# Transposing the attention weights on VectorE and through DRAM instead of on TensorE, from the fourth batch on

## The chip, the cores and the metric

The kernel runs on one NeuronCore of a Trainium2 chip. A core has a matrix engine (TensorE, "PE" in the profile; its weight loads are "PEld"), three engines for elementwise work (VectorE "DVE", ScalarE "ACT", GpSimd "POOL") and SyncE ("SP"), whose queue here issues nearly all transfers (DMA). The engines run their own instruction streams in order and wait for each other by semaphores. TensorE writes its results to PSUM, a small memory of banks; the other engines read them from there.

The metric is the device time of one execution in microseconds (us), as a median of several runs. One further execution was recorded by the hardware profiler; all times of single instructions come from it.

## The reference

All numbers are float32. There are 8 batches, 8 heads, 576 tokens and a head width of 64.

```
scores = q @ k^T / 8
attn   = exp(scores - max) where scores >= max - tau, else 0;   attn /= sum(attn)
x      = attn @ v, heads put side by side: 576 x 512 for each batch
u      = x + real(fft over tokens (fft over channels (x)))
out    = u + relu(layernorm(u) @ w_ch1) @ w_ch2          (512 -> 2048 -> 512)
```

## The kernel before

**Attention** goes by pairs of heads: 4 pairs a batch, 32 in all (`n`). The queries of a pair are cut into five steps: t = 0 to 3 have 128 queries of both heads, and t = 4 has the last 64 queries of each head, 128 rows together. So there are 20 steps a batch and 160 in all (`i`). A step computes scores on TensorE into two double banks of PSUM (tag "sc"), the negated row maximum on VectorE (L506), the exponential on ScalarE (L512), the threshold and the row sum in one VectorE instruction (L527), and, from the third batch on, scales the weights by the reciprocal sums on ScalarE (L540).

The product with v contracts over the keys, so it needs the weights with keys on the partitions. The function `weights_in_parts` does this: TensorE transposes each 128 x 128 piece of the weights `e` into PSUM (one instruction at L578 for the 64 last keys of both heads, eight at L596), and ScalarE copies the results to `e_t` and `ends` (L584, L598). For t = 4 there are five transposes, since its 128 rows share one set of keys.

`values_in_parts` then multiplies: part 0 takes the queries of t = 0 and 1, part 1 those of t = 2, 3 and 4. Each part is 20 recorded matmuls (L627).

**The mixing** (the Fourier transforms, folded by symmetry) and **the feed-forward** run behind, a batch at a time. The feed-forward takes groups of 512 tokens. From the second group on both products use a two-level fast scheme with fewer block products (Strassen's kind); their weight forms are made once, kept in DRAM (`f1`: 28 blocks, `f2`: 49 blocks of 256 KB) and streamed in for each of these eight groups. They come through a ring in the tiles `w1[0..2]`: a load takes `PER` blocks, `block` asks for a later load when it reaches the first block of one, and `ensure` issues it on SyncE's queue (L1036).

**The order** is written out by hand. From step 40 on one loop (L1635) runs the steps: scores of step `i`; values of a part; maxima and exponentials; a piece of filling (`fill`); thresholds and reciprocals; the transposes of step `i - 1`, with two more pieces of filling in and behind them; scaling of the weights. A piece of filling is mixing and feed-forward work for a fixed number of matmul columns. This number, `per_slot`, is set once a batch from the work that is left. What remains of the feed-forward runs after the last step. At t = 3 VectorE prepares q and k of the next pair by 32 x 32 block transposes (`prep_pair`, L398 to L401), at t = 2 its v is loaded, and at the end of t = 4 q and k of the pair after next are (L134: eight transfers of 72 KB in runs of 128 bytes). At the end of each batch, VectorE folds the rows of the last pair.

`mm` is a set of four PSUM banks that all other matmuls and the transposes share in turn. Each bank has to be emptied by ScalarE or VectorE before TensorE can use it again.

The code that the change touches, with what calls it:

Of the kernel before, what the change touches and what calls it, by code (L numbers as in the profile page):

```python
# [47 lines left out]
def kernel(  # L48
# [18 lines left out]
    NT = 5  # L67
# [29 lines left out]
    v_in = [const.tile([128, 10, D], FP32, name=f"v_in{u}") for u in range(2)]  # L97

# [158 lines left out]
    w1 = [const.tile([128, HID], FP32, name=f"w1_{c}") for c in range(ND)]  # L257
# [181 lines left out]
    def softmax(i, between=None, meanwhile=None, behind=None):  # L439
# [43 lines left out]
        if normalized(i // NT):  # L483
            nc.vector.tensor_scalar(
                out=e[:, 0:S], in0=e[:, 0:S], scalar1=den[:, 0:1], scalar2=None, op0=ALU.mult
            )
            if nh == 2:
                nc.scalar.activation(
                    out=e[:, S : 2 * S], in_=e[:, S : 2 * S], func=ACT.Copy, scale=den[:, 1:2]
                )  # L490
        else:
            rec = sb.tile([128, 2 * D], FP32, tag="rec", name="rec")
            nc.gpsimd.tensor_copy(
                rec[:, :].rearrange("p (j d) -> p j d", j=nh), _repeated(den[:, 0:nh], 2 * D // nh)
            )
# [51 lines left out]

    def transposed_weights(i):
        for _ in weights_in_parts(i):
            pass  # L550

    def weights_in_parts(i):

        n, t = divmod(i, NT)
        e, rec = steps.pop(i)
        if t in (0, 2):

            e_t = sb.tile([128, 8, S - 256], FP32, tag="e_t", bufs=1, name="e_t")  # L560
            ends = sb.tile([128, 2, S - 256], FP32, tag="ends", bufs=1, name="ends")
            vt = heads[n][2]
            if t == 0 and PAIRS[n % NPAIR] % 2:

                vt = sb.tile([128, 10, D], FP32, tag="vr", bufs=1, name="v_rev")
                src = heads[n][2]
                nc.gpsimd.tensor_copy(vt[:, :, 0:1], src[:, :, 0:1])
                last = src[:, :, D - 1 : D]
                down = bass.AP(
                    tensor=last.tensor, offset=last.offset,  # L570
                    ap=[list(last.ap[0]), list(last.ap[1]), [-1, D - 1]],
                )
                nc.gpsimd.tensor_copy(vt[:, :, 1:D], down)
            heads[n] = (*heads[n][0:2], vt, e_t, ends)
# [5 lines left out]
        if rec is not None:  # L580
            nc.tensor.transpose(pe[:, 1, :], rec[:, :], ident[:, :])
            kept = 2
# [22 lines left out]
    def values_in_parts(n, part):  # L605
# [19 lines left out]
        for c in range(5):  # L625
            for j in range(2):
                nc.tensor.matmul(  # L627
                    pv[64 * j : 64 * j + 64, 0:m], vt[:, 2 * c + j, :],
                    e_t[:, 4 * j + c, 0:m] if c < 4 else ends[:, 0, 0:m],
                    start=(c == 0), stop=(c == 4), skip_group_check=True,  # L630
                )
        yield
        if normalized(n):
# [238 lines left out]
    def channels(rows):  # L872
# [18 lines left out]
        def both():  # L891
            yield from w1_forms()
            ensure(1)
            while not next(forms_w2):
                yield
# [32 lines left out]
    def w1_forms():  # L928
# [36 lines left out]
        ensure(0)  # L965
# [60 lines left out]
    PER = 4  # L1026
    LOADS = [(f1, 28, k) for k in range(0, 28, PER)] + [(f2, 49, k) for k in range(0, 49, PER)]
    issued = 0

    def ensure(n):  # L1030

        nonlocal issued
        while issued <= n and issued < (NG - 1) * len(LOADS):
# [3 lines left out]
                out=w1[issued % 3][:, 0 : 512 * n_blocks].rearrange("p (j n) -> p j n", n=512),  # L1037
# [4 lines left out]
    def block(g, second, index):  # L1042

        n = len(LOADS) * (g - 1) + (7 if second else 0) + index // PER
        if index % PER == 0:
            ensure(n + 2 if g > 1 or second or index < 20 else n + 1)
        return w1[n % 3][:, 512 * (index % PER) : 512 * (index % PER + 1)]

# [586 lines left out]
    for i in range(2 * per_batch, total + 3):  # L1635
# [6 lines left out]
        if t == 3 and i < total:  # L1642
# [8 lines left out]
        next(values, None)  # L1651
        if i % per_batch == 2:
# [6 lines left out]
        while held:  # L1659
            held.pop(0)()  # L1660
        if mixes:
# [82 lines left out]
```

## Time and profile before

| | |
|---|---|
| median of three runs | 1605.9 us (1603.56 to 1607.93) |
| profiled execution | 1605.7 us, span from first to last instruction 1603.8 us |
| busy in it | PE 1537.4, PEld 1189.2, DVE 1105.6, ACT 908.4, POOL 811.7 us |
| mean granted TensorE clock | 0.988 of full speed |
| transferred | 239.05 MB, 149 GB/s over the span |
| transposes into `pw` (L596) | 1152 instructions, 172.1 us busy |
| their copies to `e_t` (L598) | 256 instructions, 148.5 us busy |

The page of the profile lists the engines' busy time, then the span in 40 slices (each digit is a busy share in tenths), the transfer queues, the chain of work that ended last, the costliest groups of instructions, and the transfers. A group's line names the source line, engine and operation, output and inputs, shapes and count; then the busy time in us and the mean ns of one; then how long its engine sat idle just before them, and what ended that wait. Busy time of overlapping instructions is counted once. The queue rows of SyncE show how long it was held by issuing, waits of the instructions merged in a row included.

### The profile page before, as it was taken

The page shows a single profiled execution, that of the slowest core. Times are in us where ns is not written, and L with a number is a line of the kernel's source. Part 1 is how long each engine was busy: PE and PEld are TensorE (multiplying, and loading weights), DVE is VectorE, ACT ScalarE, POOL GpSimd, SP SyncE. Part 2 cuts the span into 40 slices and gives each one's busy share as a digit, 9 for nine tenths or more (in the row PEclk, how much of TensorE's full clock was granted, in tenths as well). Part 3 has the DMA queues.
Part 4 walks back from the last instruction along what each step waited for, and adds up shares of the span by engine and source line. Part 5 has one row for each costly group of instructions (what it writes and reads, how often), then busy time and mean ns, then how long its engine had stood idle before and what let it go on. Part 6 is the DMA issues. An engine that isn't in the chain of part 4 may idle for free.

```text
span 1603.8 us, 27061 instructions
## 1 busy us (share of the span) xinstructions
PE 1537.4 (96%) x9770; PEld 1189.2 (74%) x9770; DVE 1105.6 (69%) x2165; ACT 908.4 (57%) x1873; POOL 811.7 (51%) x1014
## 2 busy tenths in 40 slices
PE   8999979999999999999999999999999999999997
PEld 4555445555787778877787878787887778879997
DVE  7997886845869566766577566856676656746547
ACT  5774665554655666656666666656665665223121
POOL 6784664034455552536254724455263625537646
PEclk9999999999999999999999999999999999999998
DMA  6423221555956264634564355626463534546655
GB/s 158 131 57 115 75 76 36 175 158 164 291 159 203 72 182 125 182 104 141 141 175 140 113 159 145 191 69 180 123 185 108 154 113 158 191 157 237 235 193 190
DMA packets 245499, 239.05 MB, mean 149 GB/s; under 512 B 196947, under 2 KB 214869, under 8 KB 225014
## 3 DMA queue, kind: packets, MB, share of 16 engines
q1 hardware_dynamic: 242854, 237.02, 49.1%
q8 instruction: 78, 1.28, 0.3%
q10 hardware_dynamic: 2512, 0.30, 0.2%
q14 instruction: 55, 0.45, 0.1%
HBM read 207.50 MB, written 29.62 MB: 148 GB/s over the span
## 4 chain that ended last, share of the span: by engine, by line
PE 76%; DVE 14%; ACT 4%; issue 2%; POOL 2%; DMA 1%; SPq 0%; DVEq 0%; ACTq 0%; POOLq 0%
PE ph L1163 24%; PE po L1306 17%; PE pv L627 8%; PE sc L427 7%; PE pw L596 6%; PE po L901 4%; PE ph L877 2%; PE py L750 2%; DVE e L467 2%; PE sc L433 1%; PE pa L767 1%; PE pe L578 1%; PE pa L771 1%; DVE neg L451 1%; ACT e L512 1%
## 5 line engine op out<-in xcount | busy, mean ns | idle before, releaser
L512 ACT ACTIVATE e<-sc,neg 128x576 f32<-128x576 f32 x216 | 158.6, 734 | 139.8 <-DVE neg L506 139.4
L506 DVE TENSOR_REDUCE neg<-sc 128x1 f32<-128x576 f32 x216 | 154.0, 749 | 112.0 <-PE sc L427 104.1
L1306 PE MATMUL po<-w,w_all 128*128 128x128 f32 x1792 | 229.1, 278 | 0.7 <-ACT ends L584 0.7
L1306 PEld LDWEIGHTS po<-w,w_all 128*128 128x128 f32 x1792 | 214.7, 193 | 10.2 <-issue 5.5
L1100 DVE TENSOR_TENSOR hs<-ph,hs 128x512 f32<-128x512 f32 (+1 forms) x128 | 105.1, 821 | 158.5 <-PE ph L1163 104.0
L1109 POOL TENSOR_TENSOR w<-hs 128x512 f32<-128x512 f32 x32 | 42.1, 1320 | 318.9 <-ACT hs L1105 245.1
L596 PE MATMUL pw<-ident,e 128*128 128x128 f32 x1152 | 172.1, 276 | 18.0 <-ACT x_first L634 9.1
L1163 PE MATMUL ph<-u_t,w 128*128 128x256 f32 x768 | 180.5, 381 | 0.5 <-DMA w<-f 0.4
L527 DVE SCALAR_TENSOR_TENSOR e<-sc,thr,e 128x576 f32<-128x576 f32 x216 | 168.1, 811 | 17.7 <-ACT thr L516 17.7
L427 PE MATMUL sc<-kT,qT 64*128 64x288 f32 x1024 | 170.3, 432 | 7.9 <-DVE e L467 7.9
L598 ACT COPY e_t<-pw 128x512 f32<-128x512 f32 x256 | 148.5, 594 | 45.8 <-PE pw L596 44.6
L540 ACT ACTIVATE e<-e,den 128x576 f32<-128x576 f32 x216 | 157.6, 775 | 16.6 <-DVE den L534 15.4
L596 PEld LDWEIGHTS pw<-ident,e 128*128 128x128 f32 x1152 | 136.3, 142 | 36.3 <-ACT x_first L634 10.1
L1163 PE MATMUL ph<-w_all,w 128*128 128x256 f32 x672 | 157.0, 382 | 2.9 <-DVE hs L1100 1.8
L1163 PEld LDWEIGHTS ph<-u_t,w 128*128 128x128 f32 x768 | 141.2, 190 | 23.4 <-issue 4.4
L1105 ACT ACTIVATE hs<-hs 128x512 f32<-128x512 f32 (+1 forms) x96 | 74.1, 772 | 122.0 <-DVE hs L1100 120.8
L1163 PEld LDWEIGHTS ph<-w_all,w 128*128 128x128 f32 x672 | 123.5, 190 | 25.6 <-issue 6.2
L427 PEld LDWEIGHTS sc<-kT,qT 64*128 64x128 f32 x1024 | 93.9, 186 | 62.9 <-issue 32.8
L1213 POOL TENSOR_TENSOR w_all<-w_all 128x128 f32<-128x128 f32 (+2 forms) x160 | 118.5, 758 | 29.9 <-DVE w_all L1326 22.4
L1306 PE MATMUL po<-w,hs 128*128 128x128 f32 x960 | 126.3, 279 | 0.0
L1306 PEld LDWEIGHTS po<-w,hs 128*128 128x128 f32 x960 | 116.2, 193 | 9.4 <-issue 7.2
L792 POOL TENSOR_TENSOR u_t<-x,tmp 128x289 f32<-128x289 f32 (+1 forms) x45 | 34.5, 766 | 104.8 <-DVE tmp L787 104.8
(221 smaller groups left out, 2985.1 us busy)
## 6 DMA issues: line engine op xcount, KB each, us to landing
w<-f SPq DMA_DIRECT2D x152, 1024.0 KB, 4.9
hs<-in_moe_w_ch_dram SPq DMA_DIRECT2D x23, 512.0 KB, 4.6
q_in<-in_q_dram SPq DMA_DIRECT2D x128, 72.0 KB, 3.9
out_dram<-u SPq DMA_DIRECT2D x36, 256.0 KB, 2.5
k_in<-in_k_dram SPq DMA_DIRECT2D x124, 72.0 KB, 3.0
v_in<-in_v_dram SPq DMA_DIRECT2D x64, 128.0 KB, 4.7
f<-w SPq DMA_DIRECT2D x14, 512.0 KB, 4.0
f<-w SPq DMA_DIRECT2D x7, 1024.0 KB, 4.4
```

The costliest lines, as they stand in the source:

```text
L427: nc.tensor.matmul(sc[j][:, c, 0:HALF], qT[hp, 128 * t : 128 * t + 128], kT[hp, k0 + HALF * c : k0 + HALF * (c + 1)], start=True, stop=True,)
L506: nc.vector.tensor_reduce(out=neg[:, j : j + 1], in_=sc[j][:, :, 0:HALF], axis=AXIS_XY, op=ALU.max, negate=True,)
L512: nc.scalar.activation(out=ej, in_=sc[j][:, :, 0:HALF], func=ACT.Exp, bias=neg[:, j : j + 1], scale=1.0)
L527: nc.vector.scalar_tensor_tensor(out=ej, in0=sc[j][:, :, 0:HALF], scalar=thr[:, j : j + 1], in1=ej, op0=ALU.is_ge, op1=ALU.mult, accum_out ...
L540: nc.scalar.activation(out=e[:, S * j : S * (j + 1)], in_=e[:, S * j : S * (j + 1)], func=ACT.Copy, scale=den[:, j : j + 1],)
L596: nc.tensor.transpose(pw[:, c, :], e[:, c0 : c0 + 128], ident[:, :])
L598: nc.scalar.copy(e_t[:, 4 * j : 4 * j + 4, qs], pw[:, :, :])
L627: nc.tensor.matmul(pv[64 * j : 64 * j + 64, 0:m], vt[:, 2 * c + j, :], e_t[:, 4 * j + c, 0:m] if c < 4 else ends[:, 0, 0:m], start=(c == 0 ...
L1100: nc.vector.tensor_tensor(out=to, in0=bank, in1=to if other is None else other, op=ALU.add)
L1163: nc.tensor.matmul(bank[:, 256 * q : 256 * q + 256].rearrange("p (two n) -> p two n", two=2), left[:, 256 * c + 128 * q : 256 * c + 128 * ...
L1213: return lambda: eng.tensor_tensor(out=to, in0=to, in1=other, op=ALU.add)
L1306: nc.tensor.matmul(to, lefts[m][j][:, s], right_[:, 128 * s : 128 * (s + 1)], start=(jn in (0, 4) or cut and jn > 4) and s == 0, stop=s == ...
```

## The change

From pair 12 on (the fourth batch; `by_dma`) the steps t = 0 to 3 transpose their weights without TensorE. In the next step of the loop, VectorE transposes each 32 x 32 block of `e` in two instructions (640 columns behind the maxima, 512 behind the thresholds) into one room of 1152 columns, `et_room`. It lies in the second half of `w1[2]`, which grows by 128 columns. A transfer then stores the room into one of three DRAM buffers in turn (590 KB, rows of 4608 bytes). A step later four transfers read it back, one for each 32 partitions, so that the blocks come to the right partitions (runs of 1152 bytes). They land in `et_all`, which holds three such pieces and takes the place of `e_t`, `ends` and `rec` in the SBUF. The step t = 4 keeps its five transposes on TensorE, and ScalarE copies their results into `et_all`.

With it move: part 0 of the values runs at t = 4 instead of t = 3; its and part 1's right operand is read in runs of 32 columns; part 1 has the queries of t = 4 first and is copied out by two instructions. The ring for the feed-forward's weights has five rooms of two blocks instead of three of four blocks, and the loads are asked for four ahead instead of two.

The core of the diff:

```diff
+    et_all = const.tile([128, 3 * SLOT], FP32, name="et_all")        # SLOT = 4 * 9 * 32
+    by_block = et_all[:, :].rearrange("p (blk c q) -> p blk c q", c=NC9, q=32)
...
+    et_room = w1[2][:, HID // 2 : HID // 2 + 4 * 9 * 32]
...
+    def by_dma(n):
+        return n >= 3 * NPAIR
...
+    scratch = [dram.tile([128, SLOT], FP32, name=f"e_blocks{u}") for u in range(3)]
+
+    def blocks(i, part):
+        n, t = divmod(i, NT)
+        if i < 0 or i >= B * NPAIR * NT or not by_dma(n) or t == 4:
+            return
+        e = steps[i][0]
+        c0, c1 = ((0, 5), (5, NC9))[part]
+        out_ = et_room.rearrange("p (b c q) -> p c b q", b=4, c=NC9)
+        nc.vector.transpose(out_[:, c0:c1], e[:, 128 * c0 : 128 * c1])
+        if part == 1:
+            steps.pop(i)
+            nc.sync.dma_start(out=scratch[i % 3][:, :], in_=et_room)
+
+    def fetch(i):
+        n, t = divmod(i, NT)
+        if i < 0 or i >= B * NPAIR * NT or not by_dma(n) or t == 4:
+            return
+        at = SLOT * (0, 1, 1, 2)[t]
+        src = scratch[i % 3][:, :].rearrange("(a p) (b m) -> b p a m", p=32, b=4)
+        for b in range(4):
+            nc.sync.dma_start(
+                out=et_all[32 * b : 32 * b + 32, at : at + SLOT].rearrange(
+                    "p (a m) -> p a m", a=4
+                ),
+                in_=src[b],
+            )
...
     def weights_in_parts(i):
         n, t = divmod(i, NT)
+        if by_dma(n) and t < 4:
+            if t == 0:
+                heads[n] = (*heads[n][0:2], v_of(n), None, None)
+            return
...
+                if by_dma(n):
+                    at = 4 if c == 4 else 5 * j + c
+                    right = by_block[:, 0:8, at, :] if part == 0 else by_block[:, 2:12, at, :]
...
+        if by_dma(n) and part == 1:
+            nc.scalar.copy(x[:, 512:S], pv[:, 0:64])
+            nc.scalar.copy(x[:, 256:512], pv[:, 64:m])
...
-    PER = 4
+    PER = 2
...
+    def ring(n):
+        room = n % 5
+        return w1[room // 2][:, 1024 * (room % 2) : 1024 * (room % 2) + 1024]
...
-        n = len(LOADS) * (g - 1) + (7 if second else 0) + index // PER
+        n = len(LOADS) * (g - 1) + (14 if second else 0) + index // PER
         if index % PER == 0:
-            ensure(n + 2 if g > 1 or second or index < 20 else n + 1)
+            ensure(n + 4 if g > 1 or second else min(n + 4, 13 if index < 24 else 15))
...
         if i < total:
             scores(i)
-        if t == 3 and i < total:
+        if t == (4 if by_dma(n) else 3) and i < total:
             values = values_in_parts(n, 0)
...
             softmax_first(i)
         next(values, None)
+        fetch(i - 2)
+        blocks(i - 1, 0)
...
             softmax_second(i)
         while held:
             held.pop(0)()
+        blocks(i - 1, 1)
```

`v_of(n)` is the former code for the reversed copy of v, moved into a function of its own. `LOADS` counts 14 and 25 loads for `f1` and `f2` after the change, where it counted 7 and 13.

## The prediction

> **What bounds the kernel now.** I read the page first: busy time, the 40 slices, and the chain that ended last.
>
> ```profile
> PE 1537.4 (96%) x9770; PEld 1189.2 (74%) x9770; DVE 1105.6 (69%) x2165; ACT 908.4 (57%) x1873; POOL 811.7 (51%) x1014
> ...
> PEclk9999999999999999999999999999999999999998
> ...
> PE 76%; DVE 14%; ACT 4%; issue 2%; POOL 2%; DMA 1%; SPq 0%; DVEq 0%; ACTq 0%; POOLq 0%
> ```
>
> TensorE is the bound: it is full in nearly every slice, holds three quarters of the chain, and has its clock. So I cut out the stretch that the change touches, from the last scores of pair 11 (471.6 us) to those of pair 31 (1346.5 us): 20 pairs of five steps, 43.75 us a pair. The second view is a table of this stretch (span, PE, PEld, DVE, ACT, POOL, clock, DMA share, GB/s), then the same for the two lines of transposes (PE, PEld, and then clock, DMA share and GB/s of the whole).
>
> ```profile
> 471.60:1346.50 874.90, 856.20 (x5900) 699.68 (x5899) 591.50 (x1194) 557.62 (x1154) 420.81 (x546) 0.99 0.49 143
> 471.60:1346.50 874.90, 111.15 (x720) 86.76 (x720) 0.99 0.49 143
> 471.60:1346.50 874.90, 27.91 (x100) 14.14 (x100) 0.99 0.49 143
> ```
>
> TensorE idles 18.7 us of 874.9; VectorE is 68% busy and the DMA engines 49%. There is room on both, but not much.
>
> **What it removes.** Of every five steps, four lose 9 transposes each (one of the ends, L578, and eight, L596): 720 in 80 steps. Their matmul time contains pipeline ends that overlap the next work, so I take the weight loads, which space them: 86.76 x 640/720 + 14.14 x 80/100 = 88.4 us, or 4.4 us a pair. A pair falls to 39.3 us if nothing else waits. ScalarE loses three copies a step (two of 594 ns, one of 297): 80 x 1.49 = 119 us. It was not the bound, so I cost that at nothing in time.
>
> **What it adds on VectorE.** Two block transposes a step, of 640 and 512 columns. The nearest rows:
>
> ```profile
> L398 DVE STREAM_TRANSPOSE kT<-k_in 128x576 f32<-128x576 f32 x32 | 24.8, 776 | 4.1 <-DMA k_in<-in_k_dram 3.9
> ...
> L399 DVE STREAM_TRANSPOSE kT<-k_in 64x64 f32<-64x64 f32 x32 | 7.8, 243 | 0.4
> ```
>
> From 64 to 576 columns 533 ns are added, 1.04 ns a column over a base of 0.18 us: 0.84 and 0.71 us, 1.55 a step, 124 us in all. No row shows the scattered output (32 columns at a time). I take the plain price. Bounds: the plain price, and a doubled one, another 124 us. VectorE then has 591.5 + 124 = 716 us of work against TensorE's 786: 91%, close behind the bound.
>
> The Trainium skill, page "VectorE: DVE Perf Modes", section "Rules for kernel authors", speaks against the change: for a 128x128 transpose it recommends TensorE where a PSUM destination is acceptable, and VectorE's transpose only within blocks of 32. By that rule alone the sum would be VectorE's 124 us for TensorE's 88, a loss of 36; but these are two engines, and only the bound's time counts here.
>
> **What it adds in transfers.** A step stores its 590 KB in rows of 4608 B and fetches them by four transfers in runs of 1152 B. The rows to price them (landing times of the 512 KB and 256 KB stores, minimum, median and maximum; then single microseconds in the order of the table above; then SyncE's queue):
>
> ```profile
> DMA to landing us min/median/max: 3.2/4.0/5.7
> DMA to landing us min/median/max: 2.0/2.5/3.9
> 703.00:704.00 1.00, 1.00 (x11) 1.00 (x11) 0.36 (x4) 0.92 (x3) 0.00 (x0) 1.00 1.01 153
> ...
> 717.00:718.00 1.00, 1.00 (x9) 0.38 (x6) 0.00 (x0) 0.53 (x2) 0.55 (x1) 1.00 0.99 418
> 699.22 2.17 SPq L134 DMA_DIRECT2D q_in<-in_q_dram  x4
> 701.43 2.12 SPq L134 DMA_DIRECT2D k_in<-in_k_dram  x4
> ```
>
> With all engines busy, loads in 8 KB rows move 418 GB/s and q and k, in runs of 128 B, 153. On one of 16 engines that is 313 and 13.4 ns a packet, a line of 8.6 ns plus 0.037 ns a byte. So a store costs 8 packets of 180 ns an engine, 1.44 us, and a fetch 32 of 51 ns, 1.65 us. For 80 steps 247 us, over 0.49 x 874.9 = 429 us now: 676 us, 77% of the present stretch. A fetch's bounds are 1.41 us (at 418 GB/s) and 3.85 (at 153). Landing of a store: 1.2 us lie between 256 and 512 KB, so 576 KB lands in 3.5 us on an empty queue.
>
> SyncE issues the store and four fetches: at the 0.54 us of q and k 2.7 us more a step. The weight ring is cut into halves, twice the transfers at 0.34 us, each still asked for 8 blocks ahead. I cost the ring at nothing: a block is eight matmuls of 128 ns (L1306) or 235 ns (L1163), so 8 blocks cover 8 to 15 us. If SyncE is held longer than that, TensorE waits at its next block.
>
> **The new waits.** The transposes write one room (`et_room`), free again only when the previous step's store has landed. Behind that wait on VectorE stand the bank additions, the thresholds, and so the next scores on TensorE, which need the score banks back. From the room being free to the next store: 0.84 + the additions of a third of the filling + thresholds 1.57 (140.91 us of L527 in 180) + denominators 0.48 + 0.71. The additions are what is left of VectorE's 591.5 us without reductions 128.3, thresholds 140.9, denominators 47.7 and preparation 35.9: 238.7 us in 300 fillings, 0.80 each. Sum 4.4 us. Then 3.5 us of landing, and 1.25 us for one 512 KB ring load ahead in the queue at 418 GB/s: 9.15 us from room to room. Bounds of the queue: nothing, and two such loads, 2.5.
>
> Against this, TensorE's steps. Values cost 2.65 us (105.83 us / 40), scores 1.25, the ends' scores 1.14, t=4's remaining five transposes 0.6. That leaves 27.3 of 39.3 us for filling, 5.45 a step: t=2 and t=3 last 6.7 us, t=4 9.25, the next t=0 7.3, t=1 9.35. Without a wait VectorE reaches the room 2.7 us after the scores start (the reductions' end, 633.55 + 1.42, in this step of the trace):
>
> ```profile
> 632.28 1.24 PE L427 MATMUL sc<-kT,qT 64*128 64x288 f32 x8
> ...
> 633.55 1.42 DVE L506 TENSOR_REDUCE neg<-sc 128x1 f32<-128x576 f32 x2 [1.19 <-PE sc L427]
> ...
> 639.53 0.79 PEld L427 LDWEIGHTS sc<-kT,qT 64*128 64x128 f32 x8
> ```
>
> Count from the scores of t=2. VectorE gets the room at 2.7 and, in t=3, at 2.7 + 9.15 = 11.85; the thresholds end 3.2 later, at 15.05, where TensorE wanted the scores of t=4 at 13.4: **1.65 us lost**. In t=4 the room comes at 21.0, but that step is long and has one head, so TensorE goes on. Its store leaves at 24.6 and lands at 29.35; the fetch of t=3 waits for it on SyncE. Meanwhile q and k are issued (4.3 us, above) and fill the engines for 4.7 us until about 31.7; the fetch's last part lands 1.65 + 1.7 us later, at 35.05 (1.7 is the landing of the 2.2 KB row swaps). TensorE wants the values of part 1 at 15.05 + 9.25 + 7.3 + 1.25 = 32.85: **2.2 us lost**. Part 0's fetch lands about as it is wanted: nothing.
>
> Two smaller terms. At a batch's end VectorE is already solid and TensorE waits for it:
>
> ```profile
> 693.48 0.30 PE L578 MATMUL pe<-ident,e 128*128 128x128 f32 x1 [2.62 <-DVE w_all L1326]
> 694.00:695.00 1.00, 0.83 (x4) 0.83 (x5) 0.96 (x5) 0.76 (x4) 1.00 (x1) 0.50 0.00 0
> ```
>
> The added 1.55 us lengthen it in five batches, 0.4 us a pair. And after that 2.62 us gap the granted clock is 0.50 in this and the next two microseconds, a loss of some 1.6 us. Stalls of 1.65 and 2.2 us are just shorter; I charge one such loss in every second pair, 0.8 (bounds: none, one in each pair). The Trainium skill, page "TensorE: Matmul & The Clock Gate", section "Why this matters for your kernels", says that the clock falls at idle gaps above about 3 us. By that rule nothing is to be charged here, and the sum would be 16 us lower; this trace shows the drop at a gap of 2.62 us with 0.85 us of idling shortly before, so the row decides.
>
> **Sum.** 43.75 - 4.4 + 1.65 + 2.2 + 0.4 + 0.8 = 44.4 us a pair, 13 us more in 20 pairs: 1605.7 + 13 = 1619 us. The profiled execution took 1605.7 us (span 1603.8) and the median of the runs is 1605.9, so nothing has to be shifted. The stretch before pair 12 and the last 257 us keep their work. Part 0 of the values moves from t=3 to t=4 of the same pair at the same cost; one more ScalarE copy a pair lies under TensorE.
>
> **The rivals.**
> - The waits are mostly hidden, TensorE stays the bound, and the kernel gets faster. Price: with an empty queue the room returns every 7.9 us, t=3 loses 0.4 us, and the fetch can land before its values: 39.7 us a pair, 81 us less, 1525; with half of the stalls some 1570. For it: DMA at 49%, ScalarE relieved of 119 us. Against it: a store's landing alone is 3.5 us of a 6.7 us step. It turns into a loss where the stalls of a pair reach 4.4 us. Chance 0.35, 1525 to 1598.
> - The transfers become the bound. If a fetch costs the 3.85 us of the q and k rate, the engines have 676 + 80 x 2.2 = 852 us of work in 875, the queue ahead of each store grows to two loads or more (room every 10.4 us, some 4 us lost in t=2 and t=3), and the values wait 3.5 us: about 47.5 us a pair, 1680. For it: fetches write 32 partitions at a time, as q and k do. Against it: nine times longer runs. A doubled price of the block transposes (VectorE 840 us) would end here too. Chance 0.25, 1635 to 1710.
> - The forecast, stalls that about eat the gain: 1598 to 1635, chance 0.40.
> That the transposes don't leave TensorE can't be: the code no longer issues them.
>
> **How the numbers follow.** 0.3% (4.8 us) is about what a measurement can tell from no change. Of the forecast's 0.40 I put 0.05 below, 0.10 within and 0.25 above it. Faster 0.35 + 0.05 = 0.40, same 0.10, slower 0.25 + 0.25 = 0.50. The range leaves out a tenth on each side: 1555 to 1675.
>
> **What would show it.** The stretch of 20 pairs at about 888 us; PE busy there near 768 us; L596's count down by 640 and ScalarE by 119 us; block transposes near 0.84 and 0.71 us; VectorE's waits led by the store into DRAM and by PE; TensorE waiting before the scores and before the values; a granted clock below 0.99; a DMA share near 0.75. The prediction is wrong on the fast side if VectorE never waits for the store, and on the slow side if the fetches land after 4 us or more, or the scattered transposes take twice their price.

## The result, and the profile after

The changed kernel takes 1800.8 us (median of four runs, 1793.91 to 1811.29) against 1606.6: a ratio of 1.122 with a 95% interval of 1.115 to 1.128. It is slower by an eighth. The forecast had the direction of its likeliest case right (1619 us, slower), but the time lies far above its range.

First the page of the changed kernel, profiled in an execution of 1805.3 us with a span of 1803.5: the engines' busy time, TensorE's granted clock in 40 slices, and the chain that ended last.

```profile
PE 1558.4 (86%) x9050; PEld 1166.0 (65%) x9050; DVE 1202.2 (67%) x2325; ACT 815.6 (45%) x1713; POOL 812.8 (45%) x1014
...
PEclk9999999999998998888889898898998899999999
...
PE 43%; DVE 20%; DMA 14%; SPq 8%; ACT 6%; POOL 5%; issue 5%; DVEq 0%; POOLq 0%; ACTq 0%
```

TensorE fell from 96% to 86% of the span. Its share of the chain fell from 76% to 43%, and transfers (DMA) and SyncE's issuing (SPq), 1% together before, are 22% of it now. The clock shows eights where the change is at work. And TensorE is busy for 21 us *longer* than before, with 720 instructions fewer.

Next a table over the same stretch as in the prediction, from the last scores of pair 11 to those of pair 31 (columns: stretch, its length, then PE, PEld, DVE, ACT and POOL busy, granted clock, DMA share, GB/s).

```profile
470.88:1533.40 1062.52, 874.32 (x5168) 676.08 (x5167) 681.35 (x1346) 463.19 (x986) 418.18 (x544) 0.90 0.73 203
```

The stretch grew from 874.9 to 1062.5 us, by 187.6. Before it and behind it lie 741 us, against 729 before. So the stretch holds nearly the whole loss. In it TensorE idles 188.2 us (18.7 before) and is busy 874.3 us (856.2 before), at a clock of 0.90 instead of 0.99. What TensorE waited for there (columns: instruction, what ended the wait, us in all, times, longest):

```profile
PE pv L702 <- DMA et_all<-e_blocks: 59.9, 17, 6.8
PE ph L1244 <- DVE hs L1181: 28.3, 8, 7.1
PE pv L702 <- DMA out_dram<-u: 17.5, 4, 5.1
PE sc L437 <- DVE e L537: 15.5, 9, 2.7
PE pv L702 <- issue: 12.9, 3, 5.9
PE ph L1244 <- POOL w_all L1294: 11.6, 2, 7.0
```

L702 is the values. All its waits together are some 101 us. Some of them the view puts down to another store or to "issue"; these at part 1 too belong to the late fetch, for they nearly vanish in a run below in which the fetch comes earlier. The scores (L437, and 9.9 us at L443) lose 25 us, and the feed-forward's first product (L1244) some 47 us behind late work of VectorE (on `hs`, its hidden tile) and GpSimd.

Part 1 has 320 columns where part 0 has 256, so that the groups by shape tell them apart (whole program; idle time behind the last bar). Part 1 waits 52.1 + 34.0 = 86 us:

```profile
L702 PE MATMUL pv<-et_all,v_in 128*64 128x320 f32 x320 | 68.0, 591 | 52.1 <-DMA et_all<-e_blocks 45.4 <-issue 5.9 <-ACT et_all L670 0.8
L702 PE MATMUL pv<-et_all,v_rev 128*64 128x320 f32 x320 | 60.5, 537 | 34.0 <-DMA out_dram<-u 17.5 <-DMA et_all<-e_blocks 6.8 <-ACT e L522 4.1
```

The transposes and the transfers themselves cost about what was forecast (two groups of instructions, then two groups of transfers with their median landing time):

```profile
L587 DVE STREAM_TRANSPOSE w<-e 128x640 f32<-128x640 f32 x80 | 67.0, 837 | 77.2 <-DMA e_blocks<-w 69.1 <-ACT e L522 6.2 <-ACT hs L1253 1.8
...
L587 DVE STREAM_TRANSPOSE w<-e 128x512 f32<-128x512 f32 x80 | 55.5, 694 | 0.0
```

```profile
e_blocks<-w SPq DMA_DIRECT2D x80, 576.0 KB, 3.5
et_all<-e_blocks SPq DMA_DIRECT2D x320, 144.0 KB, 3.5
```

So no single operation is dear. The loss is in when they happen. This is SyncE's queue around one of the waits for part 1 (start, duration, line, transfer, count):

```profile
907.51 0.34 SPq L590 DMA_DIRECT2D e_blocks<-w  x1
907.95 1.29 SPq L1117 DMA_DIRECT2D w<-f  x2
909.33 3.69 SPq L141 DMA_DIRECT2D q_in<-in_q_dram  x4
913.06 3.62 SPq L141 DMA_DIRECT2D k_in<-in_k_dram  x4
916.72 1.92 SPq L600 DMA_DIRECT2D et_all<-e_blocks  x4
```

and TensorE at the same time:

```profile
916.72 1.24 PE L437 MATMUL sc<-kT,qT 64*128 64x288 f32 x8
922.52 5.45 PE L702 MATMUL pv<-et_all,v_in 128*64 128x320 f32 x20 [4.57 <-DMA et_all<-e_blocks]
```

The store of t = 3 is issued at 907.5 and lands at about 912. The fetch that reads it back is issued only at 916.7, because the eight loads of q and k for the pair after next hold SyncE for 7.3 us. TensorE finishes the scores at 917.96 and waits 4.57 us. Then the values run for 5.45 us. Two microseconds at a time (columns as in the table above) show why they take so long:

```profile
918.00:920.00 2.00, 0.00 (x0) 0.00 (x0) 1.90 (x4) 0.08 (x1) 0.00 (x0) 1.00 0.96 226
920.00:922.00 2.00, 0.00 (x0) 0.00 (x0) 1.81 (x3) 1.47 (x3) 0.00 (x0) 0.72 0.90 214
922.00:924.00 2.00, 1.48 (x6) 0.86 (x8) 0.00 (x0) 0.00 (x0) 0.00 (x0) 0.50 1.00 367
924.00:926.00 2.00, 2.00 (x10) 1.04 (x8) 0.00 (x0) 0.00 (x0) 0.00 (x0) 0.50 0.68 270
```

After the idling the clock is granted at one half. So a wait is paid twice, once while it lasts and once in the work behind it.

### The profile page after: what moved, and what is told of

Read it like the earlier page. It is cut to its first block, busy times and chain, and to the rows that moved or that the text cites. A ratio compares the mean times of both kernels' runs of the same rounds, so it can differ in the third digit from the quotient of the medians.

```text
span 1803.5 us, 26710 instructions
## 1 busy us (share of the span) xinstructions
PE 1558.4 (86%) x9050; PEld 1166.0 (65%) x9050; DVE 1202.2 (67%) x2325; ACT 815.6 (45%) x1713; POOL 812.8 (45%) x1014
## 4 chain that ended last, share of the span: by engine, by line
PE 43%; DVE 20%; DMA 14%; SPq 8%; ACT 6%; POOL 5%; issue 5%; DVEq 0%; POOLq 0%; ACTq 0%
PE ph L1244 11%; PE pv L702 10%; PE po L1387 8%; SPq L141 5%; DMA et_all<-e_blocks 4%; DMA e_blocks<-w 4%; PE po L978 3%; DVE e L537 3%; PE sc L437 3%; DMA w<-f 2%; DVE w L587 2%; PE ph L954 2%; DVE e L477 2%; SPq L600 1%; PE pw L666 1%
## 5 line engine op out<-in xcount | busy, mean ns | idle before, releaser
L437 PE MATMUL sc<-kT,qT 64*128 64x288 f32 x1024 | 185.4, 442 | 25.0 <-DVE e L537 15.5
L1244 PE MATMUL ph<-w_all,w 128*128 128x256 f32 x672 | 166.9, 402 | 42.5 <-DVE hs L1181 29.8
L1244 PEld LDWEIGHTS ph<-w_all,w 128*128 128x128 f32 x672 | 130.2, 199 | 76.3 <-POOL w_all L1294 26.9
L1244 PE MATMUL ph<-u_t,w 128*128 128x256 f32 x768 | 176.9, 382 | 2.8 <-POOL u_t L869 2.7
L587 DVE STREAM_TRANSPOSE w<-e 128x640 f32<-128x640 f32 (+1 forms) x160 | 122.5, 766 | 77.2 <-DMA e_blocks<-w 69.1
L702 PE MATMUL pv<-et_all,v_in 128*64 128x256 f32 (+1 forms) x640 | 112.2, 510 | 68.1 <-DMA et_all<-e_blocks 58.4
L1244 PEld LDWEIGHTS ph<-u_t,w 128*128 128x128 f32 x768 | 143.4, 190 | 30.6 <-issue 7.4
L437 PEld LDWEIGHTS sc<-kT,qT 64*128 64x128 f32 x1024 | 102.2, 191 | 86.2 <-issue 54.1
L702 PE MATMUL pv<-et_all,v_rev 128*64 128x256 f32 (+1 forms) x640 | 107.3, 492 | 41.7 <-DMA out_dram<-u 17.5
L702 PEld LDWEIGHTS pv<-et_all,v_in 128*64 128x64 f32 x640 | 57.6, 169 | 118.8 <-issue 93.4
L1387 PE MATMUL po<-w,hs 128*128 128x128 f32 x960 | 133.7, 290 | 0.6 <-DMA w<-f 0.5
L1387 PEld LDWEIGHTS po<-w,hs 128*128 128x128 f32 x960 | 123.4, 203 | 13.0 <-issue 10.7
```

What stands on the lines that cost most here:

```text
L437: nc.tensor.matmul(sc[j][:, c, 0:HALF], qT[hp, 128 * t : 128 * t + 128], kT[hp, k0 + HALF * c : k0 + HALF * (c + 1)], start=True, stop=True,)
L587: nc.vector.transpose(out_[:, c0:c1], e[:, 128 * c0 : 128 * c1])
L702: nc.tensor.matmul(pv[64 * j : 64 * j + 64, 0:m], vt[:, 2 * c + j, :], right, start=(c == 0), stop=(c == 4), skip_group_check=True,)
L1244: nc.tensor.matmul(bank[:, 256 * q : 256 * q + 256].rearrange("p (two n) -> p two n", two=2), left[:, 256 * c + 128 * q : 256 * c + 128 * ...
L1387: nc.tensor.matmul(to, lefts[m][j][:, s], right_[:, 128 * s : 128 * (s + 1)], start=(jn in (0, 4) or cut and jn > 4) and s == 0, stop=s == ...
```

## The experiments

**The theories.** *Theory Q*: the fetch is issued late on SyncE's in-order queue, behind q and k, and TensorE waits for it at part 1. *Rival R*: the one room is the cause; VectorE waits for the store, and everything behind it is late. *Rival T*: the traffic is the cause; too many bytes in too short runs. *Rival K*: the waits are small, and the clock that they cost is the loss. *Rival W*: the ring with its smaller rooms. The forecasts quoted below have letters of their own: theory A, theory D and "queue theory" there are Q, theory B and "room theory" are R, and theory C is T; "wait theory" says that the waits for the fetch are the loss, by whatever cause they are late. All experiments change the kernel after, except the ring alone, which changes the kernel before. Each ratio below is to the kernel before in the same comparison (medians from 1605.3 to 1607.4 us).

### A ladder: leaving parts out

Neither transposes nor transfers, so that `et_all` is never filled by these steps and the values of t = 0 to 3 are computed from old data:

```diff
-        nc.vector.transpose(out_[:, c0:c1], e[:, 128 * c0 : 128 * c1])
-            nc.sync.dma_start(out=scratch[i % 3][:, :], in_=et_room)
     def fetch(i):
+        return
```

> As the kernel without transfers, and VectorE's block transposes left out as well (nothing transposes the weights of t=0 to 3 from pair 12 on; the values there are computed from stale weights). This is the price of the removed TensorE and ScalarE work alone. If VectorE's 124 us are what eats the rest of the gain in the kernel without transfers (1579 us): 1517 to 1540 us. If the 88 us were priced too high: 1565 us or more.

Measured: 1555.9 us, ratio 0.9685 (0.9672 to 0.9698). The time lies between the two forecasts. This is the gross gain of the change, some 51 us, before it has paid for anything.

With VectorE's transposes, without transfers (the values read old data):

```diff
-            nc.sync.dma_start(out=scratch[i % 3][:, :], in_=et_room)
     def fetch(i):
+        return
```

> Leaves out the store and the fetches, so that the values from pair 12 on are computed from stale weights; everything else stays. This is what the change is worth without its transfers and the waits for them. Theories A, B and C alike: TensorE's 88 us are gained and little is lost, 1520 to 1550 us. If VectorE's 124 us of block transposes are the loss instead: 1600 us or more.

Measured: 1579.1 us, 0.983 (0.981 to 0.985). This again lies between the two forecasts. VectorE's 122 us of block transposes cost 23 us of time.

With the stores, without the fetches (the values read old data):

```diff
     def fetch(i):
+        return
```

> Keeps the block transposes and the store (so VectorE still waits until the room is free) and leaves out the four fetches; the values from pair 12 on are computed from stale weights. Theory A: most of the loss is in waiting for the fetch, so 1545 to 1610 us. Theory B: most of the loss stays, 1680 us or more. Theory C: half of the new traffic is gone, some 1650 us.

Measured: 1626.8 us, 1.013 (1.011 to 1.015). No theory's forecast fits. The stores cost another 48 us. VectorE waits 44 us for the room in the trace, and TensorE 17 us for VectorE at `hs` (0.3 us without stores) and 8 us for the ring's weights (none without stores).

With the fetches too, but into a place that nobody reads (the values read old data; for the space the ring has four rooms, asked for three ahead, and the last 32 of each 288 columns are not fetched):

```diff
-                out=et_all[32 * b : 32 * b + 32, at : at + SLOT].rearrange("p (a m) -> p a m", a=4),
-                in_=src[b],
+                out=w1[2][32 * b : 32 * b + 32, 0:1024].rearrange("p (a m) -> p a m", a=4),
+                in_=src[b][:, :, 0:256],
-        room = n % 5
+        room = n % 4
```

> The fetches are issued as in the changed kernel, in the same places, but land (256 of each 288 columns, 8/9 of the bytes) in a place that nobody reads, so TensorE does not wait for them; the values from pair 12 on are computed from stale weights. To make the place, the weight ring has four rooms instead of five, asked three ahead. This has the fetches' traffic and their hold on SyncE's queue, and not the wait. Wait theory (TensorE's waiting before the values, with its clock, is most of the 174 us between stores alone and the whole change): 1635 to 1670 us. Queue and traffic theory (the fetches delay stores and weight loads on the queue and the engines): 1730 us or more.

Measured: 1689.0 us, 1.052 (1.050 to 1.053). This lies between the two forecasts. The fetches cost 62 us although TensorE never waits for one. Some half of that may be the smaller ring of this experiment, for which TensorE waits as follows in the stretch (8 us with stores alone and five rooms); how the rest divides between traffic and the hold on the queue isn't shown.

```profile
PE po L1385 <- DMA w<-f: 31.5, 22, 3.1
```

From here to the changed kernel, 1800.8, are another 112 us (more by some 30, since the changed kernel has the larger ring): what it costs that TensorE has to wait for the fetches. Here is the same stretch of the ladder's ends, without transposes and transfers, and with unread fetches (columns as before):

```profile
472.06:1296.40 824.34, 792.32 (x5168) 631.82 (x5167) 595.47 (x1191) 463.37 (x989) 425.31 (x544) 0.98 0.57 152
```

```profile
474.43:1428.00 953.57, 832.70 (x5168) 651.22 (x5167) 681.91 (x1348) 465.01 (x988) 419.49 (x545) 0.95 0.80 222
```

TensorE runs the same 5168 matmuls in both and in the changed kernel. They take 792 us at a clock of 0.98, 833 at 0.95 and 874 at 0.90. So of the 238 us between 824.3 and 1062.5, 82 are slower matmuls and 156 idling. The DMA share falls from 0.80 with unread fetches to 0.73 in the changed kernel, and yet that is the slower one: the engines are not the bound (rival T as the bound falls; as a term of the loss it stays).

### The ring alone

The kernel before with five rooms of two blocks, asked for four ahead:

```diff
-    PER = 4
+    PER = 2
+    def ring(n):
+        room = n % 5
+        return w1[room // 2][:, 1024 * (room % 2) : 1024 * (room % 2) + 1024]
```

> The kernel before with only the ring changed: five rooms of two blocks, loads asked for four ahead. I costed it at nothing: 1600 to 1611 us. If the doubled number of transfers on SyncE's queue costs something by itself: 1615 us or more.

Measured: 1607.2 us, 1.0008 (0.9997 to 1.0018), ten runs. Rival W falls.

### q and k out of the way of part 1

q and k asked for at the end of the next pair's t = 1, behind both parts of the values:

```diff
-        if t == 4 and n + 2 < B * NPAIR:
-            load_pair(n + 2)
+        if t == 1 and 2 * NPAIR < n < B * NPAIR - 1:
+            load_pair(n + 1)
```

> The loads of q and k of the next pair but one move from the end of t=4 to the end of the next t=1, so that the fetch of t=3 is no longer issued behind them on SyncE's queue. Theory A (the fetch of t=3 comes too late because it stands behind 7.3 us of q and k issues; TensorE idles some 4.3 us before part 1 of the values and then runs at half clock): part 1's waits fall from 86 us to under 30, most of the clock loss goes with them, 1680 to 1710 us. Theory B (the single room that the block transposes write keeps VectorE and so TensorE late): 1780 us or more. Theory C (the transfers as such are too much traffic): 1780 us or more.

Measured: 1780.2 us, 1.107 (1.104 to 1.110): 21 us better only, where theory Q had promised 1680 to 1710. Part 1's wait fell from 86 to 18 us, as theory Q has it, but the delay came back somewhere else. SyncE's queue in this kernel:

```profile
564.13 1.18 SPq L729 DMA_DIRECT2D swap<-x  x2
566.45 1.37 SPq L731 DMA_DIRECT2D x<-swap  x2
567.87 2.19 SPq L141 DMA_DIRECT2D q_in<-in_q_dram  x4
570.11 2.32 SPq L141 DMA_DIRECT2D k_in<-in_k_dram  x4
572.48 2.00 SPq L600 DMA_DIRECT2D et_all<-e_blocks  x4
...
575.05 0.38 SPq L590 DMA_DIRECT2D e_blocks<-w  x1
```

VectorE finished the room at 563.74. The store is issued at 575.05: ahead of it stand the two halves of a row swap, which wait for GpSimd, and then q and k and a fetch. VectorE and TensorE then:

```profile
581.45 0.84 DVE L587 STREAM_TRANSPOSE w<-e 128x640 f32<-128x640 f32 x1 [11.74 <-DMA e_blocks<-w]
```

```profile
583.02 3.75 PE L1244 MATMUL ph<-w_all,w 128*128 128x256 f32 x8 [11.11 <-DVE hs L1181]
```

VectorE waits 11.74 us for the room and TensorE 11.11 us for VectorE. VectorE's wait for the store rose from 68 to 143 us in the stretch, and TensorE's wait for `hs` from 28 to 80.

One step earlier, at the end of t = 0:

```diff
-        if t == 4 and n + 2 < B * NPAIR:
-            load_pair(n + 2)
+        if t == 0 and 2 * NPAIR < n < B * NPAIR - 1:
+            load_pair(n + 1)
```

> The loads of q and k move to the end of the next t=0: behind the fetch of t=3, and with no store due for half a step and no fetch for more than one. Queue theory (it is the order on SyncE's queue that makes fetch and store late): part 1's waits stay below 25 us as with q and k after t=1, VectorE's wait for the room falls below 80 us from 144, 1700 to 1740 us. If the place of q and k doesn't matter beyond what the first move gave: 1770 to 1800 us.

Measured: 1719.1 us, 1.070 (1.067 to 1.073), 82 us better than the changed kernel. What TensorE and VectorE wait for in the stretch:

```profile
PE sc L437 <- DVE e L537: 27.2, 14, 3.4
PE pv L702 <- DMA et_all<-e_blocks: 23.1, 12, 4.1
```

```profile
DVE w L587 <- DMA e_blocks<-w: 85.6, 28, 6.9
```

Part 1's waits are 18 us here too, and the wait for the room is 86 us against 68 in the changed kernel. So theory Q holds for 82 us of the loss, eight small loads in the wrong place on one queue. For the rest this run doesn't show it.

### Two rooms

The store of a step need not have landed before the next step's transposes (for the space, the ring has four rooms, asked for three ahead):

```diff
+    et_rooms = [w1[2][:, 1152 * u : 1152 * (u + 1)] for u in range(2)]
+        et_room = et_rooms[t % 2]
-        room = n % 5
+        room = n % 4
```

> Two rooms for the block transposes, taken in turn (the ring gives up its fifth room for it and asks three ahead). Room theory: VectorE no longer waits for the store of the step before; the 48 us between no transfers and stores alone go, and what VectorE's lateness costs TensorE: 1730 to 1755 us. If the single room only hides behind the wait for the fetch: within 10 us of the changed kernel, 1790 to 1810 us.

The same, with q and k at the end of t = 0 as above:

> Two rooms, and q and k loaded at the end of t=0. If the wait for the room and the place of q and k on the queue are separate causes, their gains add, 1640 to 1690 us; if one takes the place of the other, this is no better than the better of the two alone.

Measured: two rooms alone 1809.3 us, 1.127 (1.123 to 1.130); with q and k at t = 0 as well 1719.6 us, 1.070 (1.068 to 1.072). VectorE's wait for the store is gone in both (from 68 us to 2 or less in the stretch), and nothing is gained. With two rooms alone TensorE waits in the stretch:

```profile
PE pv L703 <- DMA et_all<-e_blocks: 101.4, 24, 8.1
PE po L1388 <- DMA w<-f: 26.0, 20, 3.1
```

The waits at the scores and for `hs` have left the list, and those for the fetch took their place. With q and k at t = 0 as well, part 1 waits 9 us only, but part 0 waits 86 (24 in the changed kernel), 6 to 9 us at a time in half of the pairs. The fetch of t = 1, which part 0 needs one step after it is issued, still has to wait for its store and for its turn on the queue. The ring's 26 us are a price of the experiment itself. So rival R falls as the main cause: the room and the fetch are two links of one chain, and to loosen one link tightens the next. With a fifth ring room beside the two it might gain some of the 26 us; that wasn't tried.

### The clock by itself

Four matmuls of 512 columns with a result that nobody reads, ahead of part 1 of the values, to fill its wait:

```diff
+        if by_dma(n) and part == 1:
+            pd = ps.tile([128, 4, 128], FP32, tag="mm", bufs=4, name="pd")
+            for _ in range(4):
+                nc.tensor.matmul(pd[:, :, :], ones[:, :], four, start=True, stop=True)
```

> Adds four matmuls of 512 columns on the constant tile, whose results nobody reads, ahead of part 1 of the values of each pair from 12 on (some 3.5 us of TensorE work in each place where it idles some 4.3 us on average). If the drop of the clock after the idle gap costs what the records suggest, the dummy work lies in the gap, the clock stays up, and the time falls to 1720 to 1760 us. If the clock is not the cause of the slow matmuls (but contention for memory is), nothing is gained: 1795 us or more.

Measured: 1772.4 us, 1.104 (1.101 to 1.108). That is 28 us faster than without them, although they are 74 us of extra work (by the groups, then TensorE's timeline, in which the four stand as eight records; the bracket gives the idling ahead):

```profile
L700 PE MATMUL pd<-ones 128*128 128x512 f32 x160 | 73.9, 604 | 0.0
```

```profile
641.81 3.70 PE L700 MATMUL pd<-ones 128*128 128x512 f32 x8
646.26 2.91 PE L709 MATMUL pv<-et_all,v_in 128*64 128x320 f32 x20 [0.75 <-DMA et_all<-e_blocks]
```

Behind the filled gap the 20 matmuls take 2.91 us instead of 5.45. The stretch's clock rises from 0.90 to 0.94, and TensorE's busy time in it is 912 us, 838 without the 74. So the real matmuls got 36 us faster by work that computes nothing. This shows the clock as a cause of its own. The gain is smaller than the expected one: 46 us of slower matmuls are left (838 against 792 without transposes and transfers), and the waits for VectorE and GpSimd and at the scores stand in this trace as before. Rival K holds for a part.

### Another queue

Store (first edit) and fetch (second, in its loop) issued by ScalarE instead of SyncE:

```diff
-            nc.sync.dma_start(out=scratch[i % 3][:, :], in_=et_room)
+            nc.scalar.dma_start(out=scratch[i % 3][:, :], in_=et_room)
...
-            nc.sync.dma_start(
+            nc.scalar.dma_start(
```

> The store and the four fetches are issued on ScalarE's queue instead of SyncE's; the same transfers, the same room, nothing else moved. Theory D (what costs most is that the round trip is issued in order on SyncE's one queue, behind weight loads, row swaps and q and k that wait for other engines): VectorE's wait for the room returns to the level of the kernel with stores alone, 45 us or less instead of 69 to 144, TensorE's waits before the values fall below 35 us, and the time is 1630 to 1690 us. Theory C (the transfers as such are too much for the 16 engines, 73% busy): 1740 us or more.

Measured: 1841.2 us, 1.146 (1.144 to 1.147), 40 us slower still. The forecast gave such a time to theory C, too much traffic; but the DMA engines' share in the stretch is 0.71, no higher than in the changed kernel. ScalarE's timeline, its queue rows among it:

```profile
886.86 4.62 ACTq L600 DMA_DIRECT2D et_all<-e_blocks  x4
892.38 0.34 ACTq L590 DMA_DIRECT2D e_blocks<-w  x1
892.77 0.59 ACT L1402 COPY w_all<-po 128x512 f32<-128x512 f32 x1 [7.01 <-DMA et_all<-e_blocks]
```

The fetch waits for landings, and ScalarE, which issues it, waits with it. Seven microseconds pass until it copies the next bank out. Only about 1 us of them is the wait for the store. The program gives its transfers eight completion semaphores in turn, whatever their queue, and the next holder of a semaphore waits until the last one has landed: here the third of the four fetches was issued at 890.33, when a weight load of SyncE's queue had landed at 890.31. By the trace's semaphores ScalarE waits in this way for some 137 us in the stretch, against 22 us for the landing of stores; on SyncE's queue the changed kernel loses some 13 us so. Theory Q in the form "any queue without q and k will do" falls: a transfer that waits must not stand ahead of work. The Trainium skill, page "DMA: Bandwidth & Descriptors", section "Issuing engines are not separate DMA queues", says that issuing from several engines saves only the time that it takes to initiate a transfer. This run agrees that it buys little, and shows a cost that the sentence leaves out, the wait ahead of the issue. A queue with no other work, and with semaphores of its own, was not tried, so what an ideal queue would give stays open.

### Two steps of lead

Only t = 0 and t = 2 go by VectorE and DRAM (the first edit stands in `blocks` and in `fetch`); t = 1 and t = 3 are transposed by TensorE and copied by ScalarE into `et_all`. Every fetch then has two steps until its values, as those of t = 0 and t = 2 had before, and the room is used every second step at most:

```diff
-        if i < 0 or i >= B * NPAIR * NT or not by_dma(n) or t == 4:
+        if i < 0 or i >= B * NPAIR * NT or not by_dma(n) or t not in (0, 2):
...
-        if by_dma(n) and t < 4:
+        if by_dma(n) and t in (0, 2):
```

> Only t=0 and t=2 go through VectorE and DRAM; t=1 and t=3 are transposed by TensorE and copied by ScalarE into the same block layout. The room then has two steps to come free and each fetch two steps to land, with half of the traffic. Theory D and the room theory both say that nearly all waits go: TensorE's half of the gain (44 us) less half of what the kernel without transfers lost, 1575 to 1605 us. Theory C: half of the loss stays, 1680 to 1710 us.

The same with store and fetch on ScalarE's queue, as above:

> As the kernel with t=0 and t=2 alone, and store and fetches on ScalarE's queue. If SyncE's queue still costs something there, this is 5 to 20 us faster than with SyncE, 1570 to 1600 us; if two steps of lead hide it, the two agree within 5 us, or this one is slower by what ScalarE's issuing (some 2 us a step in two of five) costs.

Measured: on SyncE's queue 1598.5 us, ratio 0.9943 (0.9931 to 0.9956), faster than the kernel before by 0.6%, a small difference but one beyond the interval; the same from ScalarE's queue 1703.3 us, 1.060 (1.058 to 1.061), far outside its forecast. The stretch of the first:

```profile
472.00:1337.10 865.10, 830.79 (x5531) 666.57 (x5530) 634.28 (x1274) 509.48 (x1111) 423.84 (x544) 0.99 0.69 198
```

Neither VectorE waits for the room nor TensorE for a fetch; idling is 34 us and the clock 0.99. The DMA share, 0.69, is close to the changed kernel's 0.73. So transfers of this kind can be hidden. The half version has more lead and also half of the stores and fetches; which of the two counts for more these runs don't tell apart. Less traffic and more lead together are still not enough: from ScalarE's queue even the half version loses 97 us against the kernel before. There TensorE doesn't wait for a fetch but for ScalarE, which empties its banks (54.6 us for the copies to `et_all`).

Two variants of it. In the first pair of each batch, where VectorE folds the previous batch's rows, all steps stay on TensorE:

```diff
-        if by_dma(n) and t in (0, 2):
+        if by_dma(n) and t in (0, 2) and n % NPAIR > 0:
```

> The version with t=0 and t=2 alone, but the first pair of each batch, in whose steps VectorE is solid, is transposed by TensorE throughout (and has part 0 of its values at t=3). If the batch end limits that version: 1588 to 1596 us. If not: some 8 us of TensorE time come back, 1598 to 1608 us.

And the half version with q and k at the end of t = 0:

> The version with t=0 and t=2 alone, with q and k loaded at the end of t=0. With two steps of lead the fetches should not care: 1594 to 1602 us, the same as without. If SyncE's order still costs there: 1585 to 1592 us.

Measured: 1597.8 us, 0.9942 (0.9926 to 0.9958), and 1597.0 us, 0.9940 (0.9928 to 0.9952). Neither can be told from the half version. So neither run shows the batch end or SyncE's order as its limit. The place of q and k, worth 82 us in the full change, is worth nothing measurable in the half version.

## Why the prediction was wrong, by its steps

In its own units, us a pair, the prediction was 44.4; the stretch took 1062.5 / 20 = 53.1. The missing 8.7 are split evenly: idling, where 4.25 was added and (188.2 - 18.7) / 20 = 8.5 came, and matmul time, where it had 768 us + 0.8 a pair, 39.2 a pair, and 874.3 / 20 = 43.7 came.

- **"4.4 us a pair" removed.** Mis-sized. By the weight loads 88.4 us were to leave TensorE. The run without transposes and transfers has 64 us less of busy time (856.2 to 792.3) and is 51 us faster: 2.5 a pair. Even without a wait for transfers, VectorE would have taken 23 of the 51.
- **"The added 124 us" on VectorE.** Right: 122.5 us, 0.84 and 0.69 us each. The scattered output costs nothing.
- **Landing, ring, ScalarE.** The store's landing of 3.5 us was right. The ring at nothing was right in the kernel before (1.0008). ScalarE lost 93 us of work instead of 119, at no gain, as forecast.
- **"1.65 us lost" before the scores.** The size is about right, 25 us in the stretch, 1.3 a pair, but largely by luck. The prediction had this stall at t = 4 in every pair, behind the room. There (L443) TensorE waited 4 times in 20 pairs, 9.9 us. And the run without transfers, in which the room is always free, has 18 us of waits at the scores too (14.9 at L437, 3.5 at L443).
- **"2.2 us lost" before part 1.** The mechanism was right: q and k on SyncE's queue ahead of the fetch of t = 3. The size was wrong: 86 us, 4.3 a pair. I took q's and k's issuing from one place, 4.3 us. On average the eight took 5.8 us in the very stretch before (0.73 us each by SyncE's rows), and 7.2 in the stretch after. The place was typical, for the median load took 0.49 us before; but some took up to 3 us, and they make the mean. (The 4.7 us for which q and k were to fill the engines have no working either: 590 KB at the row's 153 GB/s are 3.9 us.)
- **"Part 0's fetch lands about as it is wanted: nothing."** Wrong by 1.1 us a pair (22 us in the stretch, at the groups of 256 columns). A fetch that is just in time on paper is late in some of the pairs.
- **VectorE's lateness.** The wait for the room was followed to the scores only. It reached the feed-forward too: its products wait some 47 us for VectorE and GpSimd, 2.4 a pair, against 0.4 that was charged at the batch's end. With two rooms the waits for `hs` and `w_all` are gone (0.3 us of 40), so they do come from the room; 7.5 us behind GpSimd stay. The prediction named the bank additions behind that wait, and then did not ask who waits for them.
- **The clock, "one such loss in every second pair, 0.8".** The largest error: against the run without transposes and transfers the same matmuls took 82 us more, 4.1 a pair, more than the upper bound of one loss in each pair. The trace has 37 spells at half clock in the stretch, 222 us in all, where the stretch before has 4 with 14 us. What failed is less the rule than the stalls that it was applied to. They were not one of 1.65 and one of 2.2 us a pair: where part 1 waited it was mostly for 4 to 7 us. Shorter ones came close together. These are rows of the changed kernel's timeline:

```profile
956.05 1.21 PE L443 MATMUL sc<-kT,q_ends 128*128 128x288 f32 x4 [1.63 <-DVE e L537]
958.90 3.80 PE L702 MATMUL pv<-et_all,v_rev 128*64 128x256 f32 x20 [1.65 <-DMA w<-f]
...
979.01 2.91 PE L702 MATMUL pv<-et_all,v_rev 128*64 128x320 f32 x20 [1.55 <-ACT e L522]
...
994.90 3.29 PE L1244 MATMUL ph<-t_room,w 128*128 128x256 f32 x8 [2.13 <-POOL t_room L1168]
...
1013.48 2.38 PE L702 MATMUL pv<-et_all,v_rev 128*64 128x256 f32 x20
```

Behind two gaps of 1.63 and 1.65 us, with 1.21 us of work between them, the 20 matmuls take 3.80 us instead of 2.38; the granted clock over 956 to 962 us is 0.72. A gap of 1.55 us by itself costs nothing (2.91 us, as behind the filled gap above). One of 2.13 us by itself does: the 8 matmuls take 3.29 us, where 16 such matmuls just before took 3.72. The prediction weighed a rule of the Trainium skill at this place (page "TensorE: Matmul & The Clock Gate", section "Why this matters for your kernels": no idle gaps above about 3 us). The measurement decides against it here, for gaps of less than 3 us cost clock. By the rule the sum was to fall by 16 us; the clock cost 82.

- **The rivals.** "The waits are mostly hidden" fell: its point of return was 4.4 us of stalls a pair, and 8.5 came. "The transfers become the bound" gave the nearest time of the three (1635 to 1710), but by another cause: fetches landed in 3.5 us and not in more than 4, the engines were busy at 0.73, as the forecast said (near 0.75), and a higher share in other runs went with a shorter time. Of the signs that the prediction named for its slow side, median landings of 4 us or more and transposes at twice their price, neither came.

So the steps that failed are the length of the stall before part 1, the clock behind the stalls, and the waits that were put at nothing, at part 0 and in the feed-forward. The range failed with them because both ends treated the terms one by one. They aren't independent, as the moves of q and k and of the room show: each wait makes the work behind it slower and the next issue later, so that these errors point the same way.

## What to carry to other kernels

Before moving work off the bound onto a round trip through memory, write down how many steps lie between the last input and the first use, and want slack beyond the landing times: with one step of lead at half of its fetches this change cost 12%; with two at all, and half of the transfers, it gained 0.6%. On an in-order queue look at what stands ahead of each transfer that somebody waits for, a swap or eight small loads included, with mean times and not with one row; and don't put a transfer that waits ahead of an engine's own work. Charge each regular gap of TensorE of 2 us or more, and shorter ones that come close together, with the half-speed work behind it as well as with itself.

## What the runs showed of the hardware

- In the changed kernel's stretch, gaps of TensorE that stood alone (no other above 0.3 us in the 6 us ahead) were never followed by half clock up to 1.6 us, always above 3.2 us, and in seven of twelve cases between 2.1 and 3.1 us. Two gaps of 1.63 and 1.65 us close together were. After a gap of 4.57 us the 20 matmuls of 320 columns took 5.45 us, against 2.91 in the run with the gap filled. Matmuls without use in the gap made the kernel 28 us faster.
- Issuing has a long tail: half of the loads of q took 0.49 us of SyncE's time or less before, but single ones of q and k up to 3 us, and the mean was 0.73 us before and 0.90 after. It isn't shown to grow with the traffic: with q and k at t = 1 the mean was 0.75 in the same traffic (208 against 203 GB/s). The store, with 4.6 KB rows, took 0.35.
- A block transpose whose output is scattered in runs of 32 columns costs what a plain one does: 0.84 us for 640 columns and 0.69 for 512; the plain one of 576 columns had taken 0.78.
